# Text queries formed inside the key stage of a two-stream attention block, with the text columns and transposes one group earlier and the key casts given fixed engines

## The chip, the cores and the metric

The kernel runs on one core of one Trainium2 chip. The metric is the device time of one execution in microseconds (us), lower is better. A core has a matrix engine (TensorE, called PE in the profile, with its weight loads listed apart as PEld), VectorE (DVE), ScalarE (ACT), GpSimd (POOL) and SyncE (SP, which here only issues DMA transfers). Each engine runs its own instructions in the order in which the program lists them, and waits on semaphores for the others.

## The reference

Two batches of 256 image tokens and 32 text tokens with D = 1152 features go through one joint attention block. Everything is bfloat16.

```
mod_i = (silu(c) @ wmod_img).reshape(B, 6, 1, D)      # shift, scale, gate used; same for text
hi = layernorm(x_img) * (1 + sci) + shi
ht = layernorm(x_txt) * (1 + sct) + sht
qi, ki, vi = split(hi @ wqkv_img);  qt, kt, vt = split(ht @ wqkv_txt)
q, k, v = concat([text, image], tokens)
p = softmax(q @ k^T * D ** -0.5);   a = p @ v;   at, ai = split(a)
out_i = x_img + gai * (ai @ wo_img)
out_t = x_txt + gat * (at @ wo_txt)
```

## The kernel before

Features are cut into KT = 9 tiles of 128. `hT_i` holds the normed image tokens transposed (features on partitions, 512 tokens), `hT_t` the same for the 64 text tokens. The order on every engine is the order in which the program is written; there is no scheduler. The stages on TensorE follow one another: warm-up, image values together with the image scale columns, image shift columns, image queries, image keys, text queries, text keys, image scores, text scores with the gate rows, text values, transposes of the probabilities, attention times values, then the output products.

Image queries and image keys come out of `qk_img(wq, blk, hooks)`. It walks over seven groups of output tiles: tiles 0 to 2 together, then 3, 4, 5, 6, 7 and 8 alone. A group is 9 matmuls of 128x512 per tile (line 481), each with its own weight load, into one PSUM bank per tile; then the bank is cast to bfloat16 into `qT` or `kT` (line 484). `hooks` maps a tile number to a function that is called ahead of that group, so what the hook issues stands on each engine just before the group's matmuls. In the key stage the hooks are:

- 3, `txt_norm`: the layer norm of the text tokens `x_t` on VectorE and ScalarE, the low part of a shift sum (line 456), and a dummy exponential on ScalarE that has the table loaded early (line 519).
- 6, `row_strips`: three strips of rows on TensorE (text shift `tsh`, text scale `tsc`, and `svr`, the image shift through the value weights), each cast out of PSUM. `svr` goes on through GpSimd to a DRAM scratch and back into `v_t`.
- 7, `all_cols`: six tiny matmuls that turn the strips into columns `ctp`, and four small VectorE instructions that write them to `mod_t` (lines 392 and 394).
- 8, `txt_transposes`: nine matmuls that transpose `x_t` (line 534, tile `tpt`, two PSUM banks), two VectorE products with the scale columns (line 535) and one VectorE addition of the shift columns (line 537), which finishes `hT_t`.

After the last group come the text queries and then the text keys: for each, 81 matmuls of 128x64 with `hT_t` as the moving operand (line 548), in two PSUM banks of 6 and 3 tiles, each cast once. A cast of queries is a ScalarE multiplication by the softmax scale (line 431); other casts go through `evac`, which takes VectorE and ScalarE in turn (lines 156 and 158). By that turn the image key casts of tiles 0, 2, 4 and 7 are on ScalarE and those of 1, 3, 5, 6 and 8 on VectorE, with `tsh` and `svr` on ScalarE and `tsc` on VectorE.

PSUM has one pool `ps_mm` of seven banks handed out in turn, and one bank `ps_sm`. Weights come in tiles of 2592 KB through a pool of five, all issued by SyncE in one fixed order (lines 412 to 422: image keys, text shift, text scale, `x_t`, text queries, text keys, image gate, text values in three parts, image output, text gate, text output in three parts); a load waits until the last reader of the tile whose place it takes is done, and the loads behind it in the queue wait with it.

Of the kernel before, what the change touches and what calls it, by code (L numbers as in the profile page):

```python
# [14 lines left out]
def kernel(  # L15
# [14 lines left out]
    nc = tc.nc  # L30
# [4 lines left out]
    B, NI, D = x_img.shape  # L35
# [19 lines left out]
    act = ctx.enter_context(tc.tile_pool(name="act", bufs=1))  # L55
# [17 lines left out]
    def load_w(src, c0, ksplits=((0, KT),), home=None):  # L73
        t = wpool.tile([P, KT, D], bf, tag="w", name="t") if home is None else act.tile([P, KT, D], bf, tag=home, name="w_home")
        for (k0, k1) in ksplits:
            nc.sync.dma_start(t[:, k0:k1, :], w_view(src)[:, k0:k1, c0:c0 + D])
        return t
# [73 lines left out]

    evac_idx = [0]

    def evac(out_ap, in_ap):
        if evac_idx[0] % 2 == 0:
            nc.vector.tensor_copy(out_ap, in_ap)
        else:
            nc.scalar.copy(out_ap, in_ap)  # L158
        evac_idx[0] += 1
# [191 lines left out]
    def v_rest_out(i0, i1, ps):  # L351
        evac(v_i[:, i0:i1, NM:D], ps[:])
# [14 lines left out]
    def strip_rows(wt, lhs):  # L367
        gps = ps_mm.tile([P, RC + P], f32, tag="mm")
        for kt in range(KT):
            for g in range(NGG):  # L370
                nc.tensor.matmul(gps[32 * g:32 * g + 32, 0:RC], lhsT=lhs[:, kt, :], rhs=wt[:, kt, g * RC:(g + 1) * RC],  # L371
                                 start=(kt == 0), stop=(kt == KT - 1), tile_position=(0, 32 * g))
        for kt in range(KT):
            g = kt % NGG
            nc.tensor.matmul(gps[32 * g:32 * g + 32, RC:RC + P], lhsT=lhs[:, kt, :], rhs=wt[:, kt, NGG * RC:D],
                             start=(kt < NGG), stop=(kt + NGG >= KT), tile_position=(0, 32 * g))
        return gps

    def rows_for_cols(wt, nm, lhs=None):
        gps = strip_rows(wt, sT32 if lhs is None else lhs)  # L380
        g_sb = work.tile([P, RC + P], bf, tag={"shr": "svr", "tsc": "garow2", "tsh": "of"}[nm], bufs=1, name=nm)
        evac(g_sb[:], gps[:])
        return g_sb

    def select_cols(g_sb, cps):
        for c in range(2):
            nc.tensor.matmul(cps[:, c * NGG * B:(c + 1) * NGG * B], lhsT=g_sb[:, c * P:(c + 1) * P],
                             rhs=sel8[:].rearrange("p g b -> p (g b)"), start=True, stop=True)
        nc.tensor.matmul(cps[:, NCOL:NCOL + B], lhsT=g_sb[:, RC:RC + P], rhs=sel2[:], start=True, stop=True)

    def cols_out(dst, cps, add):
        nc.vector.tensor_scalar_add(dst[:, 0:KT - 1, :].rearrange("p (g c) b -> p c g b", c=2),
                                    cps[:, 0:NCOL].rearrange("p (c g b) -> p c g b", c=2, b=B), add)
        nc.vector.tensor_scalar_add(dst[:, KT - 1, :], cps[:, NCOL:NCOL + B], add)
# [17 lines left out]
    w_k_i = load_w(wqkv_img, D, K3)  # L412
    w_sh_t = load_w(wmod_txt, 0)
    w_sc_t = load_w(wmod_txt, D)
    nc.sync.dma_start(x_t[0:P:P // NTT, :], xt_flat[:, :])
    w_q_t = load_w(wqkv_txt, 0)
    w_k_t = load_w(wqkv_txt, D)
# [8 lines left out]
    saccs = [act.tile([P, D], f32, tag=t, name="sacc") for t in ("K", "sacc")]  # L426
    qkTs = [act.tile([P, KT, B, NTOK], bf, tag="Q", name="qT")]

    def qk_evac(out_ap, in_ap, blk):
        if blk == 0:  # L430
            nc.scalar.mul(out_ap, in_ap, SCALE)  # L431
        else:
            evac(out_ap, in_ap)

    sparts = {}

# [21 lines left out]
    def shift_strip():  # L458
        gps = ps_mm.tile([P, RC + P], f32, tag="mm")
        terms = [(n, b) for b in range(B) for n in range(2)]  # L460
        for m, (n, b) in enumerate(terms):
            for g in range(NGG):
                nc.tensor.matmul(gps[32 * g:32 * g + 32, 0:RC], lhsT=ones32[:, b, :], rhs=sparts[n, b][:, g * RC:(g + 1) * RC],
                                 start=(m == 0), stop=(m == len(terms) - 1), tile_position=(0, 32 * g))
        for g, (n, b) in enumerate(terms):
            nc.tensor.matmul(gps[32 * g:32 * g + 32, RC:RC + P], lhsT=ones32[:, b, :], rhs=sparts[n, b][:, NGG * RC:D],
                             start=True, stop=True, tile_position=(0, 32 * g))
        g_sb = work.tile([P, RC + P], bf, tag="svr", bufs=1, name="svr")
        evac(g_sb[:], gps[:])
        return g_sb  # L470

    def qk_img(wq, blk, hooks):

        groups = [(0, 3)] + [(j, j + 1) for j in range(3, KT)]
        for (j0, j1) in groups:
            if j0 in hooks:
                hooks[j0]()
            pss = [ps_mm.tile([P, B * NI], f32, tag="mm", name="qkps") for _ in range(j0, j1)]
            for kt in range(KT):
                for j in range(j0, j1):  # L480
                    nc.tensor.matmul(pss[j - j0][:], lhsT=wq[:, kt, j * P:(j + 1) * P], rhs=hT_i[:, kt, :],  # L481
                                     start=(kt == 0), stop=(kt == KT - 1))
            for j in range(j0, j1):
                qk_evac(qkTs[blk][:, j, :, 0:NI], pss[j - j0][:].rearrange("p (b n) -> p b n", b=B), blk)

    shift_products(0, 0, KT)
    shift_products(1, 0, 2)
# [8 lines left out]
    strips = {}  # L496

    def row_strips():
        strips["tsh"] = rows_for_cols(w_sh_t, "tsh")
        strips["tsc"] = rows_for_cols(w_sc_t, "tsc")  # L500
        svr = strips["svr"] = shift_strip()
        nc.gpsimd.tensor_scalar(svn[:], svr[:, RC:RC + P], -1.0, 0.0, op0=ALU.mult, op1=ALU.add)  # L502
        for b in range(B):
            nc.gpsimd.dma_start(ssc[b, :].rearrange("(q j) -> q j", q=NGG), svr[b:P:32, 0:RC])
        for g in range(2):
            for b in range(B):
                r = 32 * (2 * g + b)
                nc.gpsimd.dma_start(v_t[r:r + NT, :], ssc[b, g * VW:(g + 1) * VW].partition_broadcast(NT))
# [12 lines left out]
    def all_cols():  # L521
        ctp = ps_sm.tile([P, 2, NCOL + B], f32, tag="sm")
        for k, rows in enumerate((strips["tsh"], strips["tsc"])):
            select_cols(rows, ctp[:, k, :])
        for k in range(2):
            cols_out(mod_t[:, k, :, :], ctp[:, k, :], float(k))

    def txt_transposes():
        pick = ident[:].rearrange("p (t r) -> p r t", r=P // NTT)[:, 0, :]
        hv = hT_t[:].rearrange("p k (b t) -> p k b t", b=B)  # L530
        for k0, k1 in ((0, 5), (5, KT)):
            tpt = ps_mm.tile([P, 5, NTT], f32, tag="mm")
            for kt in range(k0, k1):
                nc.tensor.matmul(tpt[:, kt - k0, :], lhsT=x_t[:, kt * P:(kt + 1) * P], rhs=pick, start=True, stop=True)
            nc.vector.tensor_mul(hv[:, k0:k1], tpt[:, 0:k1 - k0, :].rearrange("p k (b t) -> p k b t", b=B),
                                 mod_t[:, 1, k0:k1, :].unsqueeze(3).to_broadcast([P, k1 - k0, B, NT]))
        nc.vector.tensor_add(hv, hv, mod_t[:, 0, :, :].unsqueeze(3).to_broadcast([P, KT, B, NT]))

    qk_img(w_k_i, 1, hooks={3: txt_norm, 6: row_strips, 7: all_cols, 8: txt_transposes})

    FG = 6
    for blk, wq in enumerate([w_q_t, w_k_t]):
        for j0 in range(0, KT, FG):
            jn = min(FG, KT - j0)
            ps = ps_mm.tile([P, FG, NTT], f32, tag="mm")
            for j in range(j0, j0 + jn):
                for kt in range(KT):
                    nc.tensor.matmul(ps[:, j - j0, :], lhsT=wq[:, kt, j * P:(j + 1) * P], rhs=hT_t[:, kt, :],  # L548
                                     start=(kt == 0), stop=(kt == KT - 1))
            qk_evac(qkTs[blk][:, j0:j0 + jn, :, NI:NTOK],  # L550
                    ps[:, 0:jn, :].rearrange("p j (b n) -> p j b n", b=B), blk)


    qpos = [[0, P, 2 * P], [NT, NT + P, 0]]
# [268 lines left out]
    def out_txt_mm():  # L823
        pss = [ps_mm.tile([P, VC], f32, tag="mm", name="ops") for _ in range(2)]
        for h in range(2):
            for dt in range(KT):
                for g in range(NGG):
                    nc.tensor.matmul(pss[h][32 * g:32 * g + 32, :], lhsT=aT[:, dt, NI + h:NI + NTT:2],  # L828
                                     rhs=w_o_t[:, dt, g * VC:(g + 1) * VC], start=(dt == 0), stop=(dt == KT - 1),
                                     tile_position=(0, 32 * g))  # L830
        return pss
# [19 lines left out]
    pss = out_txt_mm()  # L851
# [36 lines left out]
```

## Time and profile before

| what | value |
|---|---|
| time before, median of 3 runs | 117.55 us (117.52 to 117.86) |
| the profiled execution's own time | 117.92 us |
| its span, first to last instruction | 115.9 us |
| PE busy | 109.1 us (94% of the span), 1223 matmuls |
| DVE, ACT, POOL busy | 76.1, 38.6 and 27.6 us |
| mean DMA rate over the span | 353 GB/s, and 400 to 414 in most slices up to 98 us |
| granted TensorE clock | 0.999 |

The profiled execution is one execution, so its span plus 2.0 us around it makes its own 117.92 us, which is 0.37 us above the median of the runs. Times inside the profile are in us from the first instruction. In a chain of waits each row is a start, a length and the engine, tile and line that held the end of the kernel up at that time. "issue" is time in which an engine waited for nothing that the profile shows.

### The profile page before, as it was taken

The numbers are of one execution on the slowest core, as the hardware profiler recorded it, in microseconds if no ns is written. First come the engines' busy times: TensorE is split into PE (matmuls) and PEld (weight loads), VectorE is DVE, ScalarE is ACT, GpSimd is POOL, SyncE is SP. The second block draws the span as 40 slices with busy tenths as digits, with TensorE's granted clock in tenths as the row PEclk, the third lists the DMA queues.
The fourth block names the chain that finished last, engine by engine and source line by source line (L and its number), as shares of the span: only waits on it lengthen the run. The fifth ranks groups of instructions, "written<-read, shape, count | busy, mean of one in ns | idle before, by whom it ended". The sixth has DMA issues, their size and how long they took to land.

```text
span 115.9 us, 2913 instructions
## 1 busy us (share of the span) xinstructions
PE 109.1 (94%) x1223; PEld 64.9 (56%) x1230; DVE 76.1 (66%) x152; ACT 38.6 (33%) x91; POOL 27.6 (24%) x60
## 2 busy tenths in 40 slices
PE   5998999999999999999999999869999999999990
PEld 1354664544944444444448458857688655667660
DVE  1698920452499999999999854026665802998670
ACT  2829660343360620920039421305565700001000
POOL 7000102540130000000000406000460460799200
PEclk9999999999999999999999999999999999999999
DMA  3999999999999999999999999999999999932042
GB/s 87 270 348 371 373 382 402 410 411 413 403 411 413 405 413 405 410 413 411 411 413 414 403 410 408 405 397 408 411 407 404 407 409 400 339 148 102 25 161 68
DMA packets 22775, 40.87 MB, mean 353 GB/s; under 512 B 1311, under 2 KB 6571, under 8 KB 22763
## 3 DMA queue, kind: packets, MB, share of 16 engines
q1 hardware_dynamic: 21680, 39.64, 89.6%
q0 software_dynamic: 608, 0.88, 2.1%
q10 hardware_dynamic: 475, 0.18, 0.6%
q8 instruction: 9, 0.15, 0.5%
q14 instruction: 3, 0.02, 0.0%
HBM read 39.36 MB, written 1.34 MB: 351 GB/s over the span
## 4 chain that ended last, share of the span: by engine, by line
PE 86%; DMA 6%; SPq 2%; issue 2%; DVE 1%
PE qkps L481 30%; PE ps L810 15%; PE va L247 10%; DMA x_i<-in_x_img_dram 6%; PE aps L718 5%; PE ps L548 4%; PE sps L574 4%; PE gps L371 3%; PE ops L828 2%; PE ps L347 2%; SPq L93 2%; PE ps L398 2%; PE ps L649 2%; PE mps L207 1%; PE gps L783 1%
## 5 line engine op out<-in xcount | busy, mean ns | idle before, releaser
L481 PE MATMUL qkps<-hT_i,t 128*128 128x512 bf16 x158 | 35.4, 379 | 0.2
L481 PEld LDWEIGHTS <-t 128*128 128x128 bf16 x162 | 15.6, 98 | 18.4 <-issue 0.2
L443 DVE SCALAR_TENSOR_TENSOR sacc<-w_v_i,mod_img,sacc 128x1152 f32<-128x1152 bf16 x16 | 22.7, 1418 | 0.5
L810 PE MATMUL ps<-t,aT 128*128 128x384 bf16 x99 | 16.4, 326 | 0.0
L810 PEld LDWEIGHTS <-aT 128*128 128x128 bf16 x117 | 11.0, 98 | 6.8 <-issue 0.5
L247 PE MATMUL va<-w_v_i,hT_i 128*128 128x512 bf16 x60 | 14.1, 379 | 0.5 <-DMA w_v_i<-in_wqkv_img_dram 0.3
L816 DVE TENSOR_TENSOR tmp<-ps,gb 128x384 bf16<-128x384 f32 x11 | 6.1, 551 | 6.1 <-PE ps L810 6.1
L247 PEld LDWEIGHTS <-hT_i 128*128 128x128 bf16 x63 | 5.9, 97 | 7.0 <-POOL hT_i L231 0.5
L794 POOL TENSOR_TENSOR w_og<-t,gb 128x384 bf16<-128x384 bf16 x9 | 8.7, 996 | 4.6 <-PE ps L810 4.6
L502 POOL TENSOR_SCALAR svn<-svr 128x128 bf16<-128x128 bf16 x1 | 0.3, 300 | 32.3 <-ACT svr L158 32.3
L165 DVE BATCH_NORM_STATS2 stats<-x_i 128x6 f32<-128x384 bf16 x12 | 5.9, 544 | 2.9 <-DMA x_i<-in_x_img_dram 2.9
L142 PE MATMUL wps<-wz 128*128 128x512 bf16 x16 | 6.5, 562 | 1.2 <-DVE wz L127 1.2
L431 ACT ACTIVATE qT<-qkps 128x512 bf16<-128x512 f32 x9 | 4.9, 596 | 6.4 <-PE qkps L481 6.4
L447 ACT CAST shi<-sacc 128x1152 bf16<-128x1152 f32 x2 | 2.3, 1152 | 13.7 <-DVE sacc L443 13.7
L548 PE MATMUL ps<-hT_t,t 128*128 128x64 bf16 x162 | 5.1, 193 | 1.4 <-issue 1.4
L231 POOL TENSOR_SCALAR hT_i<-hT_i,mod_img 128x256 bf16<-128x256 bf16 x5 | 2.5, 513 | 15.9 <-ACT rstd L172 9.3
L548 PEld LDWEIGHTS <-t 128*128 128x128 bf16 x162 | 4.9, 98 | 1.8 <-issue 1.7
L731 DVE TENSOR_SCALAR aT<-aps,sv 128x288 bf16<-128x288 f32 (+2 forms) x11 | 4.3, 455 | 2.0 <-PE aps L718 2.0
L817 DVE TENSOR_TENSOR o<-tmp,x_i 128x384 bf16<-128x384 bf16 x11 | 4.7, 426 | 0.4
L733 ACT ACTIVATE aT<-aps,sv 128x288 bf16<-128x288 f32 (+2 forms) x11 | 4.0, 468 | 2.2 <-PE aps L718 2.2
L718 PE MATMUL aps<-pT,v_i 128*128 128x288 bf16 (+2 forms) x44 | 4.8, 264 | 0.0
L574 PE MATMUL sps<-kT,qT 128*128 128x288 bf16 x36 | 4.6, 286 | 0.0
(166 smaller groups left out, 146.1 us busy)
## 6 DMA issues: line engine op xcount, KB each, us to landing
t<-in_wmod_txt_dram SPq DMA_DIRECT2D x3, 2592.0 KB, 21.9
t<-in_wqkv_img_dram SPq DMA_DIRECT2D x6, 864.0 KB, 13.1
t<-in_wqkv_txt_dram SPq DMA_DIRECT2D x2, 2592.0 KB, 18.2
t<-in_wmod_img_dram SPq DMA_DIRECT2D x3, 864.0 KB, 11.7
w_home<-in_wmod_img_dram SPq DMA_DIRECT2D x1, 2592.0 KB, 14.4
t<-in_wqkv_txt_dram SPq DMA_DIRECT2D x3, 864.0 KB, 14.0
t<-in_wo_img_dram SPq DMA_DIRECT2D x1, 2592.0 KB, 17.9
t<-in_wo_txt_dram SPq DMA_DIRECT2D x3, 864.0 KB, 15.8
```

Source lines behind the costliest of these rows:

```text
L142: nc.tensor.matmul(ps[:], lhsT=wz[:, 0:P], rhs=wz[:], start=True, stop=True)
L165: nc.vector.bn_stats(stats[0:np_, k, :], x_ap[:, k * CH:(k + 1) * CH])
L247: nc.tensor.matmul(ps[:], lhsT=hT_i[:, kt, i * P:(i + 1) * P], rhs=w_v_i[:, kt, half * VW:(half + 1) * VW], start=(kt == 0), stop=(kt == K ...
L431: nc.scalar.mul(out_ap, in_ap, SCALE)
L443: nc.vector.scalar_tensor_tensor(saccs[b][:], w_v_i[:, kt, :], ap, saccs[b][:], op0=ALU.mult, op1=ALU.add)
L481: nc.tensor.matmul(pss[j - j0][:], lhsT=wq[:, kt, j * P:(j + 1) * P], rhs=hT_i[:, kt, :], start=(kt == 0), stop=(kt == KT - 1))
L548: nc.tensor.matmul(ps[:, j - j0, :], lhsT=wq[:, kt, j * P:(j + 1) * P], rhs=hT_t[:, kt, :], start=(kt == 0), stop=(kt == KT - 1))
L574: nc.tensor.matmul(sps[:], lhsT=qkTs[0][:, ft, b, q0:q0 + P], rhs=qkTs[1][:, ft, b, :], start=(ft == 0), stop=(ft == KT - 1))
L718: nc.tensor.matmul(bank[:, off:off + c1 - c0], lhsT=lhsT, rhs=rhs, start=(first[id(bank)] == n), stop=(final[id(bank)] == n))
L794: nc.gpsimd.tensor_mul(w_og[:, dt, 0:CH], w_o_i[:, dt, NG0:D], gb[:, B - 1, NG0:D])
L810: nc.tensor.matmul(ps[:, 0:cw], lhsT=aT[:, dt, t0:t0 + P], rhs=rhs, start=(dt == DTS[0]), stop=(dt == DTS[-1]))
L816: nc.vector.tensor_mul(tmp[:, 0:cw], ps[:, 0:cw], gb[:, b, cs])
```

## The change

`evac` takes an engine, and the image key casts follow a fixed list: tiles 0, 2, 4, 5, 6 and 7 on ScalarE, tiles 1, 3 and 8 on VectorE. Against the turn before, tiles 5 and 6 move from VectorE to ScalarE; tile 7 stays there. `tsh` and `svr` are named for ScalarE and `tsc` for VectorE, as the turn had them. The transposes of the text move from the hook ahead of tile 8 to the hook ahead of tile 7, right behind the columns. The text queries become a function and move from behind the last image group to the hook ahead of it (tile 8). The text keys stay where they were. No matmul, cast or transfer is added or taken away.

```diff
-    def evac(out_ap, in_ap):
+    def evac(out_ap, in_ap, eng=None):
+        if eng is not None:
+            (nc.vector.tensor_copy if eng == "dve" else nc.scalar.copy)(out_ap, in_ap)
+            return
         if evac_idx[0] % 2 == 0:
...
-    def rows_for_cols(wt, nm, lhs=None):
+    def rows_for_cols(wt, nm, lhs=None, eng=None):
...
-        evac(g_sb[:], gps[:])
+        evac(g_sb[:], gps[:], eng)
...
-    def qk_evac(out_ap, in_ap, blk):
+    K_ENG = ("act", "dve", "act", "dve", "act", "act", "act", "act", "dve")
+
+    def qk_evac(out_ap, in_ap, blk, eng=None):
         if blk == 0:
             nc.scalar.mul(out_ap, in_ap, SCALE)
         else:
-            evac(out_ap, in_ap)
+            evac(out_ap, in_ap, eng)
...
-        evac(g_sb[:], gps[:])                      # svr, in shift_strip
+        evac(g_sb[:], gps[:], "act")
...
-                qk_evac(qkTs[blk][:, j, :, 0:NI], pss[j - j0][:].rearrange("p (b n) -> p b n", b=B), blk)
+                qk_evac(qkTs[blk][:, j, :, 0:NI], pss[j - j0][:].rearrange("p (b n) -> p b n", b=B), blk, K_ENG[j])
...
-        strips["tsh"] = rows_for_cols(w_sh_t, "tsh")
-        strips["tsc"] = rows_for_cols(w_sc_t, "tsc")
+        strips["tsh"] = rows_for_cols(w_sh_t, "tsh", eng="act")
+        strips["tsc"] = rows_for_cols(w_sc_t, "tsc", eng="dve")
...
-    qk_img(w_k_i, 1, hooks={3: txt_norm, 6: row_strips, 7: all_cols, 8: txt_transposes})
-
     FG = 6
-    for blk, wq in enumerate([w_q_t, w_k_t]):
+
+    def qk_txt(wq, blk):
         for j0 in range(0, KT, FG):
...
+    def cols_and_transposes():
+        all_cols()
+        txt_transposes()
+
+    qk_img(w_k_i, 1, hooks={3: txt_norm, 6: row_strips, 7: cols_and_transposes, 8: lambda: qk_txt(w_q_t, 0)})
+    qk_txt(w_k_t, 1)
```

## The prediction

> **What bounds the kernel now.** I read the page first.
>
> ```profile
> PE 109.1 (94%) x1223; PEld 64.9 (56%) x1230; DVE 76.1 (66%) x152; ACT 38.6 (33%) x91; POOL 27.6 (24%) x60
> ...
> q8 instruction: 9, 0.15, 0.5%
> ...
> PE 86%; DMA 6%; SPq 2%; issue 2%; DVE 1%
> ```
>
> TensorE sets the end: 86% of the chain is matmuls in program order. To reorder matmuls gains nothing by itself; only holes in PE's row count. So the next view is the chain around the change.
>
> ```profile
> 66.27 0.02 PE ctp L389
> 66.29 1.97 PE qkps L481 x9
> 68.25 0.27 PE tpt L534 x9
> 68.52 1.94 PE qkps L481 x9
> 70.47 4.55 PE ps L548 x156
> 75.01 1.41 issue
> 76.43 0.35 PE ps L548 x6
> 76.77 1.35 PE sps L574 x11
> ```
>
> From the columns on, PE has no hole except one: 1.41 us, six matmuls before the end of the text keys. A text matmul takes 4.55 / 156 = 0.0292 us, so 162 of them from 70.47 would end at 75.20; the scores start at 76.77. The hole and the refill behind it cost 1.57 us. "issue" says that no semaphore held it: both operands were there. The DMA view of 74.06 to 74.07 shows what was going on:
>
> ```profile
> DMA packets 1, 0.02 MB, mean 1638 GB/s; under 512 B 0, under 2 KB 0, under 8 KB 0
> ## 3 DMA queue, kind: packets, MB, share of 16 engines
> q8 instruction: 1, 0.02, 550.0%
> ```
>
> A 16 KB packet of the instruction queue starts at 74.07 and takes 0.88 us; PE goes on 1.48 us after its end. Narrow windows place the nine packets at 16.17, 30.35, 42.96, 65.25, 74.07, 80.09, 85.97, 91.95 and 104.55. By then PE had run 237, 523, 686, 1082, 1415, 1537, 1873, 2017 and 2238 instructions (matmuls, weight loads and waits): 2001 over eight packets, 250 each, or 256 if missing records are allowed for. So q8 brings PE's program in blocks of about 256. The hole lies ahead of instruction 1466; blocks then begin at 1466 and every 256 before and behind. I tried when a block is asked for. If that is 46 instructions before PE enters the preceding block, seven of the nine packets start 3.43 to 4.04 us later (mean 3.71). With 60 instructions it is 3.55 to 5.21, with 36 it is 2.53 to 3.84, so 46 fits best. The other two fit the same story: the packet behind the hole starts 3.66 us after PE resumed, and the last, after the weight loads had ended, after 0.83.
>
> So the hole is a code block that came late. From request to use it takes 3.65 + 0.88 + 1.48 = 6.0 us under full DMA load, and the block in use before it was nearly all text matmuls: 256 instructions are 128 pairs, 128 x 0.0292 = 3.7 us.
>
> **The change part by part.**
>
> Text queries ahead of the last image group. The same instructions stand before instruction 1466 in another order, so the block still ends six pairs before the end of the text keys. But the 128 pairs in it are now 75 of text keys, 9 of image tile 8 and 44 of text queries. Before, the request came 23 pairs ahead of the block's first, 5 pairs into the text queries: 70.47 + 5 x 0.0292 = 70.62. After, the text queries start at 68.52, where tile 8 started, and the request comes 14 pairs in: 68.93, which is 1.69 us earlier. The block is usable at 76.43 - 1.69 = 74.74. PE arrives at 68.52 + 81 x 0.0292 + 1.95 + 75 x 0.0292 = 75.02, the same time as before, since the work is only permuted. The hole closes with 0.28 us to spare. With the spread of the seven waits (0.22 less to 0.39 more than this packet's 3.65) what is left of it is 0 to 0.11. Gain 1.57, less 0 to 0.11.
>
> [...]
>
> Transposes ahead of tile 7. On PE they only change places with that group. What must hold is that `hT_t` is finished when the text queries start at 68.52, and its cover is now the 1.94 us of tile 7. The VectorE rows:
>
> ```profile
> 66.20 0.69 DVE L156 CAST kT<-qkps 128x512 bf16<-128x512 f32 x1 [0.52 <-PE qkps L481]
> 66.81 0.17 DVE L392 TENSOR_SCALAR mod_txt<-ctp 128x16 f32<-128x16 f32 x1
> ...
> 67.03 0.15 DVE L394 TENSOR_SCALAR mod_txt<-ctp 128x2 f32<-128x2 f32 x1
> 68.44 0.82 DVE L535 TENSOR_TENSOR hT_t<-tpt,mod_txt 128x320 bf16<-128x320 f32 x2 [1.25 <-PE tpt L534]
> 69.30 0.76 DVE L537 TENSOR_TENSOR hT_t<-hT_t,mod_txt 128x576 bf16<-128x576 bf16 x1
> ```
>
> After the change tile 6's cast is off this row. The columns end on PE at 66.29; with 0.05 us to VectorE (as between PE and the cast at 66.20), the four column writes take 66.34 to 66.71, the products 0.82, the addition 0.80 with its gap: 68.33. PE can start at 68.38, with 0.14 to spare. If the seven instructions did not overlap, their rows sum to 2.31 and give 68.65: a wait of 0.13. I take 0.05, range 0 to 0.15. Had tile 6 stayed on VectorE, its 0.69 us would have stood in front and cost about 0.55; the cast list is needed for this step.
>
> Casts on ScalarE. Tile 5 adds 0.57 us ahead of `tsh`: `tsh` ends at 65.3 instead of 64.82, `svr` at 65.7 instead of 65.21, and PE wants `tsh` at 65.78. Covered by 0.4 us; without that cover, one for one. Tile 6 runs at 66.2 to 66.8 on an idle ScalarE. GpSimd's strip transfers behind `svr` start 0.5 us later, and the four loads of `v_t` behind them, which landed at 77.4, land by 78.0 against a reader at 84.72. Banks: each new order of `ps_mm` takes a bank that was cast by 65 or, for the text keys, 67. Nothing.
>
> SyncE. No DMA moves in program order. Text queries end at 70.89 instead of 72.83 and tile 8 at 72.84 instead of 70.47, so at most one weight load behind them waits about 0.8 us longer than its issue at 72.05, into a queue with 22 us of landing time. Nothing.
>
> More weight switching between 64 and 512 columns: the row shows tile 8 to text at the usual pitch. 0 to 0.1, I take 0.05.
>
> What is late next: everything from the scores on moves 1.5 us up, and data may then be missing. The last third of the text values' weights lands at 81.18 (issue 67.69, 13.5 to landing); PE reads it from 84.01, then 82.45. The last third of the text output weights lands at 102.76; read at 105.37, then 103.80. The next code block: asked for when this one arrives, 74.74, plus 6.0 = 80.74, wanted at 83.20 - 1.57 = 81.63. All hold by 0.9 us or more.
>
> The sum: 1.57 - 0.05 - 0.05 - 0.05 (a mean of the rest of the hole) = 1.42 off the profiled execution's 117.92 (span 115.9 and 2.0 around it) = 116.5. That execution is 0.37 above the median of the runs, so the median goes from 117.55 to 116.1.
>
> **The rivals.**
>
> Part of the hole stays: the request runs further ahead than 46 instructions, or the packet waits over 0.3 us longer than in these rows, or text values or output weights now come last. Left standing 0.4 to 0.9: median 116.4 to 117.2. For it: a margin of 0.28 is thin. Chance 0.13.
>
> The hole isn't closed: the packets of 74.07, 80.09, 85.97 and 91.95 are 6.0 us apart, as if the loaded DMA paced them by time. Then the block comes at 76.43 whatever PE does: 117.5. Against it: 65.25 to 74.07 is 8.8, and the packet behind the hole follows PE's restart. [...] Chance 0.09.
>
> Slower, through `hT_t`: PE stops at the first text query until L537 ends. This holds the request back too, so each microsecond of wait costs one. It makes the kernel slower once the chain ends 1.9 us later than 68.38; with 2.5 us the median is 118.2. For it: four more instructions now stand on VectorE between columns and queries, and the cover fell from 0.41 (70.06 to 70.47) to 0.14. Against: VectorE's work in front, the layer norm, tile 3's cast and `tsc`, ends at 65.2, 1.1 us before the columns, and would have to be 3 us late. Chance 0.08, most of it for what I don't see.
>
> **How the numbers follow.** Forecast 0.70, with its own range 115.9 to 116.5. About 0.3%, 0.35 us, is what a measurement of this kernel can tell. The part-closed case is faster by that or more, so faster is 0.70 + 0.13 = 0.83, same 0.09, slower 0.08. The low end 115.8 allows the full 1.57 and 0.2 of the spread of runs; the high end 117.1 takes in nearly all of the part-closed case and leaves out the last two.
>
> **What would show it.** In the changed profile PE has no "issue" row over 0.2 us in the text keys, the text queries start at 68.4 to 68.7 with L537 ended just before, tile 8 runs from about 70.9, and the instruction packet that started at 74.07 starts near 72.4. Scores start at 75.2 to 75.4. A hole of the old size at the same six matmuls would break the reading of the code block; a wait of PE on DVE hT_t L537 would break the cover; waits on weights at L649 or L828 would show that the gain was handed on to the loads.

## The result and the profile after

| | before | after |
|---|---|---|
| median of 6 runs each | 117.81 us (117.52 to 118.22) | 116.40 us (116.22 to 116.69) |
| ratio after / before, 95% interval | | 0.988 (0.9854 to 0.9905) |
| profiled execution, its span | 117.92 us, 115.9 us | 116.51 us, 114.5 us |

The kernel became faster by 1.41 us, as forecast (1.42): 1.2%, where runs of one kernel spread by about 0.3% around their median. The page first: the share of "issue" in the chain that ended last went from 2% to 0%, and VectorE lost two casts to ScalarE.

```profile
span 114.5 us, 2919 instructions
...
PE 108.8 (95%) x1230; PEld 64.7 (56%) x1230; DVE 75.0 (66%) x150; ACT 39.7 (35%) x93; POOL 27.6 (24%) x60
...
PE 87%; DMA 6%; SPq 2%; DVE 1%; issue 0%
```

The chain from the transposes on (start, length, engine, tile and line):

```profile
66.26 0.29 PE tpt L539 x9
66.54 1.96 PE qkps L486 x9
68.50 2.51 PE ps L552 x81
71.01 1.94 PE qkps L486 x9
72.95 2.36 PE ps L552 x81
75.31 4.41 PE sps L585 x36
```

There is no row without a matmul in it. The scores start at 75.31 instead of 76.77, and the gain is all there: 1.46 us. The text keys run their 81 matmuls in 2.36 us without the hole; the text queries take 2.51, 0.15 more, which is a new wait. The DMA view of 72.42 to 72.44 shows the code packet that started at 74.07 before:

```profile
q8 instruction: 1, 0.02, 300.3%
q1 hardware_dynamic: 4, 0.01, 116.2%
```

It starts at 72.43 and ends at 73.39, and the first instruction of its block runs at 74.95.

VectorE's part of the timeline:

```profile
66.30 0.17 DVE L395 TENSOR_SCALAR mod_txt<-ctp 128x16 f32<-128x16 f32 x1 [1.25 <-PE ctp L392]
...
66.72 0.82 DVE L540 TENSOR_TENSOR hT_t<-tpt,mod_txt 128x320 bf16<-128x320 f32 x2
67.58 0.76 DVE L542 TENSOR_TENSOR hT_t<-hT_t,mod_txt 128x576 bf16<-128x576 bf16 x1
```

`hT_t` is finished at 68.34. PE's semaphore instruction for it runs at 68.38 and the first text matmul starts at 68.48, where 68.32 would have been the pitch of tile 7.

### The profile page after: what moved, and what is told of

It is laid out like the page before. It is cut to its first block, busy times and chain, and to the rows that moved or that the text cites. A ratio compares the mean times of both kernels' runs of the same rounds, so it can differ in the third digit from the quotient of the medians.

```text
span 114.5 us, 2919 instructions
## 1 busy us (share of the span) xinstructions
PE 108.8 (95%) x1230; PEld 64.7 (56%) x1230; DVE 75.0 (66%) x150; ACT 39.7 (35%) x93; POOL 27.6 (24%) x60
## 4 chain that ended last, share of the span: by engine, by line
PE 87%; DMA 6%; SPq 2%; DVE 1%; issue 0%
PE qkps L486 31%; PE ps L821 16%; PE va L250 11%; DMA x_i<-in_x_img_dram 6%; PE aps L729 5%; PE ps L552 4%; PE sps L585 4%; PE gps L374 3%; PE ops L839 2%; PE ps L350 2%; PE ps L401 2%; PE ps L660 2%; SPq L93 1%; PE mps L210 1%; PE gps L794 1%; PE tp L193 1%
## 5 line engine op out<-in xcount | busy, mean ns | idle before, releaser
L250 PE MATMUL va<-w_v_i,hT_i 128*128 128x512 bf16 x63 | 14.6, 379 | 0.5 <-DMA w_v_i<-in_wqkv_img_dram 0.5
L142 PE MATMUL wps<-wz 128*128 128x512 bf16 x16 | 5.6, 499 | 1.2 <-DVE wz L127 1.2
L156 DVE CAST kT<-qkps 128x512 bf16<-128x512 f32 x3 | 2.1, 686 | 4.7 <-PE qkps L486 4.7
```

Source lines behind the costliest of these rows:

```text
L142: nc.tensor.matmul(ps[:], lhsT=wz[:, 0:P], rhs=wz[:], start=True, stop=True)
L250: nc.tensor.matmul(ps[:], lhsT=hT_i[:, kt, i * P:(i + 1) * P], rhs=w_v_i[:, kt, half * VW:(half + 1) * VW], start=(kt == 0), stop=(kt == K ...
```

## The experiments

Each time is a median. Each ratio, with its 95% interval, is against the kernel before, run beside it (117.80 to 117.96 us), also where the kernel is a variant of the changed one. A pair is a weight load and its matmul, two PE instructions.

The theory: the hole is a block of PE's program that arrives late, because 256 text instructions (128 pairs of 0.0292 us, 3.7 us) run faster than a block comes (6.0 us from request to use in the kernel before); the change puts nine slow image matmuls (1.94 us) into that block's time. The rivals: something at that place in the program (an operand, a bank, a cast), or code packets paced by time.

**Only the casts.** The hooks of before, with the fixed cast engines:

```diff
-hooks={3: txt_norm, 6: row_strips, 7: cols_and_transposes, 8: lambda: qk_txt(w_q_t, 0)})
+hooks={3: txt_norm, 6: row_strips, 7: all_cols, 8: txt_transposes})
+qk_txt(w_q_t, 0)
 qk_txt(w_k_t, 1)
```

> The order of before with only the fixed cast engines. Theory: nothing, 1.000 of before within 0.3%, with the hole of 1.4 at its place. Rival (the casts free PE or VectorE somewhere on the path): 0.3 us or more faster.

Measured: 117.80, ratio 1.0013 (0.9993 to 1.0033), and a hole of 1.43 us six matmuls before the end of the text keys. The casts alone bring nothing, as expected.

**Casts and transposes, the queries late.**

```diff
-hooks={..., 7: cols_and_transposes, 8: lambda: qk_txt(w_q_t, 0)})
+hooks={..., 7: cols_and_transposes})
+qk_txt(w_q_t, 0)
 qk_txt(w_k_t, 1)
```

> The changed kernel with the text queries put back behind the last image group; the transposes stay ahead of tile 7 and the cast list stays. Theory: the critical block again holds nothing but text matmuls, the hole of 1.4 stays at the same six matmuls and the median is that of before within 0.35 us. Rival (the gain comes from earlier transposes and the cast list): median 116.4 to 116.8 and no hole.

Measured: 117.79, ratio 0.9988 (0.997 to 1.0006). `hT_t` is ready at 68.21 here, 1.9 us before it is used, and the hole stands at the same six matmuls (chain):

```profile
70.30 4.55 PE ps L552 x156
74.85 1.33 issue
76.18 0.35 PE ps L552 x6
```

So the hole isn't `hT_t` either. The gain comes with moving the queries.

**Fewer loads.** The order of before without the last five weight loads:

```diff
-    w_ga_i = load_w(wmod_img, 2 * D, home="V")
-    w_v_t = load_w(wqkv_txt, 2 * D, K3)
-    w_o_i = load_w(wo_img, 0)
-    w_ga_t = load_w(wmod_txt, 2 * D)
-    w_o_t = load_w(wo_txt, 0, K3)
+    w_ga_i, w_v_t, w_o_i, w_ga_t, w_o_t = w_sh_t, w_q_t, w_sc_t, w_k_t, w_q_t
```

> The order of before without the five last weight loads (image gate, text values, image output, text gate, text output); their readers read weights that are there already, so the outputs are not those of the reference. The weight stream then ends at about 68 us, before the critical code block is asked for. Theory (the 6.0 us from request to use are due to the loaded DMA): the packet starts within about 1 us of the request instead of 3.65, the block is usable at about 73 and the hole closes with nothing moved; span 1.4 to 1.8 below before. Rival (the hole is fixed in PE or in the program's place): it stays at six matmuls before the end of the text keys, 1.2 to 1.5 us.

Measured: 116.34, ratio 0.9871 (0.9848 to 0.9893), span 114.5. With nothing moved in PE's order, its DMA is nearly idle from 68 to 76 us, where the DMA of before moved 407 GB/s, and its chain has no hole:

```profile
DMA packets 130, 0.16 MB, mean 21 GB/s; under 512 B 64, under 2 KB 64, under 8 KB 128
```

```profile
68.60 1.94 PE qkps L477 x9
70.54 4.72 PE ps L544 x162
75.27 1.84 PE sps L570 x15
```

The packet starts at 71.72 instead of 74.07, 1.2 us after the point 46 instructions ahead of its preceding block instead of 3.65. So the block is late because of the loaded DMA; how the packet queues inside it isn't shown here.

**Moving the boundary.** Warm-up matmuls are split into smaller ones of the same total width. This adds PE instructions ahead of everything and, if the theory holds, shifts every block boundary by as many, with no other step moved.

```diff
-    warm(11)
+    warm(6)
+    warm_split(5, 4)      # five of 128x512 as 20 of 128x128: 15 pairs more
```

> The order of before, with five of the sixteen 128x512 warm-up matmuls each split into four of 128x128: 15 more matmul and weight-load pairs, 30 more PE instructions, ahead of everything, for the same warm-up columns. Nothing is moved, cast or loaded differently. Theory (the hole is a code block that comes late): every block boundary stands 15 pairs earlier in the program, the request for the critical block now comes while the image group of tile 8 runs at 0.216 us a pair, about 2 us before the old one, and the block is wanted 0.44 us earlier; the hole of 1.41 closes to 0 to 0.3 and the median falls by 1.2 to 1.6, to about 116.3, with the text queries left where they were. Rival (the hole comes from something at that place, or the gain came from moving the queries, the transposes or the casts): the hole stays, six matmuls before the end of the text keys, and the median stays within 0.35 us of before.

Measured: 118.35, ratio 1.0021 (1.0002 to 1.004). Half of it came true and half didn't:

```profile
70.42 4.11 PE ps L556 x141
74.53 1.82 issue
76.36 0.79 PE ps L556 x21
```

The hole moved by exactly 15 pairs, from behind the 156th text matmul to behind the 141st. So the hole goes with the place in PE's program and not with the work done there, as a block boundary would. But the packet started at 74.12, as before, and the hole grew by 0.41, close to the 15 x 0.0292 = 0.44 us by which the block was wanted earlier. So "requested 46 instructions ahead of the preceding block" is not the whole rule. The mended theory is an inference, as no row shows the request itself: PE's sequencer, whose rows in the profile are the instructions that wait for semaphores (PEldq), asks for the block; it runs ahead of the array but stands at an instruction that waits for a semaphore, and in this order it stands ahead of the first text matmul until `hT_t` is done (in the kernel before `hT_t` ends at 70.05, and the sequencer's instruction for it runs at 70.09).

Thirty pairs (ten warm-up matmuls split into four):

> The order of before with ten warm-up matmuls split into four each: 30 pairs, 60 PE instructions more ahead of everything. With 15 pairs the hole moved 15 pairs earlier, as the block boundary did, but its packet started at 74.12 as before and the hole grew by 0.4. Theory, mended: PE's sequencer runs ahead of the array by about 46 instructions and asks for the next block when it enters one, but it does not run past an instruction that waits for a semaphore; the first text matmul waits for hT_t until 70.06, so no request for a block that begins behind it can come before that. With 30 pairs the block begins two pairs ahead of that matmul, inside the image group of tile 8, the request no longer stands behind the wait, and comes 2 us or more earlier: no hole over 0.2 in the text matmuls; 0 to 0.5 may open in attention times values; median 116.3 to 116.9. Rival A (packets are paced by time): packet at 74.1 again, hole grown to about 2.3, median about 118.6. Rival B (the request comes a fixed 46 instructions ahead): would also close it, but is already contradicted by the 15 pairs.

Measured: 118.66, ratio 1.0059 (1.0035 to 1.0083). Missed again: the packet started at 73.81, 0.3 earlier instead of 2.

```profile
70.44 3.67 PE ps L556 x126
74.11 1.97 issue
76.08 1.22 PE ps L556 x36
```

Two pairs ahead of the waiting instruction were not enough; either the request comes some instructions into a block, or packets are paced by time after all. Two more kernels tell these apart. One is the same 30 pairs in the kernel with the early transposes, where the sequencer passes the semaphore sooner:

> The kernel with the transposes ahead of tile 7 and the text queries behind the last image group, plus the 30 pairs in the warm-up. It differs from the 30-pair kernel of before, whose hole was 1.97, only in where the transposes and the two casts stand: PE's semaphore instruction ahead of the first text matmul is passed at about 68.25 instead of 70.07. The block boundary stands at the same 126th text matmul. Theory (the block is asked for when the sequencer gets a few instructions into the preceding block, and the sequencer stands at that semaphore until hT_t is done): the request comes at 68.3 to 68.6, the packet starts at about 72, and the hole shrinks from 1.97 to 0 to 0.5; 0 to 0.4 may open in attention times values. Median 116.3 to 117.0. Rival (the packet comes at about 74 whatever the sequencer does, as in all four kernels whose text matmuls follow tile 8): packet at 73.8, hole about 2, median about 118.6.

Measured: 116.95, ratio 0.9925 (0.9898 to 0.9953). The rows of PE's sequencer at the first text matmul, first for the 30 pairs in the order of before, then with the transposes early:

```profile
L556 PEldq EVENT_SEMAPHORE  x1: 51/51/51, 70.1 to 70.1; - x1
```

```profile
L560 PEldq EVENT_SEMAPHORE  x1: 51/51/51, 68.2 to 68.2; - x1
```

The second sequencer passes the semaphore at 68.17, while its first text matmul runs at 70.06: it works almost 2 us ahead of the array. The first passes it at 70.07, 1.90 us later, and its packet starts 1.90 us later as well, at 73.81 against 71.91. At the same boundary the hole is nearly gone:

```profile
70.22 3.67 PE ps L560 x126
73.90 0.28 issue
74.18 1.22 PE ps L560 x36
```

The other is the order of before with 40 pairs, whose preceding block begins twelve pairs ahead of the waiting instruction (nine warm-up matmuls split into four, one into six, one into nine):

> The order of before with 40 pairs, 80 PE instructions, more in the warm-up. The preceding block now begins 12 pairs ahead of the first text matmul, among the transposes, clearly in front of the semaphore that waits for hT_t. Theory: the request comes at 66 to 68, no hole over 0.3 in the text matmuls; instead 0.4 to 1.0 in attention times values at about 85, where 256 instructions ahead of a boundary that has moved 40 pairs run faster than a block comes; median 116.7 to 117.4. Rival (time-paced packet at about 74): a hole of about 2.3 before the 117th text matmul, median about 119.

Measured: 117.31, ratio 0.995 (0.9921 to 0.9978). The packet starts at 69.64 and 162 text matmuls run in one row:

```profile
68.77 1.94 PE qkps L490 x9
70.71 4.72 PE ps L557 x162
```

So 40 more pairs in the warm-up take the hole of before away without moving a query: 1.97 us at 30 pairs, none at 40. Pacing by time falls. The scores start 1.33 us earlier than before (75.44 instead of 76.77), but 0.38 of that is lost again: a hole of 0.20, expected at 0.4 to 1.0, opens in attention times values, which takes 5.77 us instead of 5.39.

By the mended theory the runs with 30 and 40 pairs in the order of before also place the request. The block begins 4 instructions ahead of the waiting one with 30 pairs, and its packet came behind the wait; with 40 pairs it begins 24 ahead, and the packet came before it. So the request falls between the 4th and the 24th instruction of a block. If it comes when the array is 46 instructions ahead of the block, the sequencer's own lead over the array is about 50 to 70 instructions; that is an estimate from these runs.

The opposite on the changed kernel: 60 pairs more (`warm(2); warm_split(1, 5); warm_split(8, 8)`).

> The changed kernel, with nine of the warm-up matmuls split (one into five, eight into eight) so that 60 more pairs, 120 more PE instructions, stand ahead of everything. Theory: with the boundaries 60 pairs earlier, a block ends in the transposes of the probabilities, behind text scores, gate rows and text values, which run through 256 instructions in about 4.4 us; with 6.0 us from request to use a hole of about 1.6 us (1.2 to 2.0) opens on PE at about 83 to 85, in the transposes, with no transfer or engine to wait for, and the median rises to about 117.9 (117.5 to 118.3). Rival (the order of the text queries itself took the hole away): no hole over 0.3 and a median within 0.35 of the changed kernel's 116.4.

Measured: 118.57, ratio 1.0046 (1.0019 to 1.0073). A hole of 1.31 us, within its range, opens where the boundary was expected to be, between the transposes of the probabilities, in a kernel that has no hole in its text matmuls:

```profile
83.84 0.55 PE pk L678 x8
84.39 1.31 issue
85.71 0.34 PE pk L678 x3
```

The median is above its range of 117.5 to 118.3; the profiled execution took 118.05, and what the rest comes from is not shown.

Counted from the start of the program, 733 weight loads stand ahead of the hole in the kernel before and in every variant with a hole in its text matmuls, with 0, 15 or 30 pairs. In the kernels with 40 and 60 pairs 989 stand ahead of it, though these two holes lie in different stages. The difference is 256 pairs, 512 instructions, two blocks of 256: the holes stand at fixed places in PE's program, whatever runs there. The change is worth its 1.4 us only for the boundaries that this program happens to have.

**The cover of the transposes.** Tiles 5 and 6 back on VectorE:

```diff
-    K_ENG = ("act", "dve", "act", "dve", "act", "act", "act", "act", "dve")
+    K_ENG = ("act", "dve", "act", "dve", "act", "dve", "dve", "act", "dve")
```

> The changed kernel with the image key casts of tiles 5 and 6 back on VectorE, all else as changed. Theory: tile 6's cast of 0.69 us stands on VectorE ahead of the column writes, which begin at about 66.85 instead of 66.30; hT_t is finished 0.5 us later and PE waits for it at the first text query, 0.5 us more than in the changed kernel; the code block's hole stays closed, as the wait holds request and need back alike; median 116.9 (116.7 to 117.1). Rival (the cast list does nothing): within 0.2 of the changed kernel's 116.4.

Measured: 116.99, ratio 0.992 (0.9897 to 0.9944). The cast of tile 6 is on the chain, and PE waits 0.47 us for `hT_t`, as expected:

```profile
66.14 0.69 DVE kT L156
66.84 0.08 DVE mod_txt L395
...
68.03 0.77 DVE hT_t L542
68.80 0.14 issue
68.93 2.52 PE ps L552 x81
```

The transposes back ahead of tile 8, directly before the queries:

```diff
+    def transposes_and_queries():
+        txt_transposes()
+        qk_txt(w_q_t, 0)
-hooks={..., 7: cols_and_transposes, 8: lambda: qk_txt(w_q_t, 0)})
+hooks={..., 7: all_cols, 8: transposes_and_queries})
```

> The changed kernel with the transposes put back ahead of tile 8, so that they stand directly before the text queries with no image group between. Theory: PE has nothing to do from the last transpose at about 68.8 until the three VectorE instructions of hT_t end at about 70.3, a wait of 1.5 to 1.8 on VectorE at the first text query; the code block's hole stays closed, as request and need are held back alike; median 118.0 (117.7 to 118.3), so that the whole gain is handed back. Rival (the wait would have been there anyway inside the code block's time): 116.4 to 117.0.

Measured: 118.30, ratio 1.0048 (1.0029 to 1.0067): 0.5% slower than before. The waits of PE in this stage (engine and tile, for whom, us in total, times, longest):

```profile
PE ps L552 <- DVE hT_t L542: 1.7, 1, 1.7
```

No hole is left in its text keys; the whole gain goes into this wait. The wait holds back request and need alike: the text queries start at 70.13 instead of 68.48, 1.65 us later than in the changed kernel, and the packet at 74.10 instead of 72.43, 1.67 later.

**A version that might beat it.** The text queries behind the second matmul of tile 8's group, beside the changed kernel once more:

```diff
             for kt in range(KT):
+                if kt == 2 and j0 in mids:
+                    mids[j0]()
```

> The changed kernel with the text queries put between the second and third matmul of tile 8's group instead of ahead of it. The first two image matmuls, 0.43 us, stand between the end of hT_t's chain and the first text query. Theory: the 0.15 us that PE waits for hT_t in the changed kernel is covered, and the code block still holds seven image matmuls between text queries and keys; median 0.1 to 0.2 below the changed kernel run beside it. Rival (that 0.15 is the cost of switching between 512 and 64 columns): the same or 0.1 above.

> The changed kernel as it is, to stand beside the others on one chip: 116.4, 0.988 of before.

Measured: 116.94, ratio 0.9905 (0.9879 to 0.9932), and for the changed kernel 116.60, ratio 0.9892 (0.9871 to 0.9913). A gain of 0.1 to 0.2 was expected and didn't come; the intervals overlap, so it isn't shown to be slower either. The profile says why: the wait for `hT_t` is gone, and a hole comes back at the boundary.

```profile
66.85 2.37 PE qkps L488 x11
69.23 2.36 PE ps L554 x81
71.59 0.05 issue
71.64 1.46 PE qkps L488 x6
73.10 2.19 PE ps L554 x75
75.29 0.02 issue
75.31 0.35 PE ps L554 x6
```

The queries take 2.36 instead of 2.51, and the last six text matmuls 0.35 instead of 0.175. From tile 7's start to the scores it is 75.66 - 66.85 = 8.81, against 75.31 - 66.54 = 8.77 in the changed kernel. The two image matmuls that cover the wait are taken from the block's time: the packet starts at 73.09, in the changed kernel beside it at 72.45.

## Why the prediction was right, point by point

- **The hole is a late code block.** Right: it moves pair by pair with the boundary (156, 141, 126 matmuls), it reappears two blocks further on, and it goes when the loads go. The distance of exactly 512 instructions also settles the count of 250 a block in favour of 256. The late block cost 1.57 us of PE in the kernel before under its full weight stream; without that stream no hole was left in the text matmuls.
- **When it is asked for.** The number was right and the rule too simple. The packet was forecast near 72.4 and started at 72.43, 3.57 us after the array came within 46 instructions of the block. One reading was loose: 5 pairs into the text queries of before is 70.42, where the 3.65 is counted from, and not 70.62, as the first text matmul starts at 70.30 and not at the chain's 70.47; the shift of 1.69 came out as 1.64. And by the mended theory the distance of 46 instructions only holds where the sequencer is free. In the kernel of before and in the changed one the block begins 28 and 37 pairs behind the waiting instruction, so that the wait did not bind; with 13 pairs (15 added in the warm-up) it did, and the packet started at 74.12, as before.
- **Gain of 1.57, less 0 to 0.11.** The hole closed entirely, but with less to spare than the 0.28 forecast: the packet ended at 73.39, and with the 1.48 us of before from there to the first instruction the block was usable at 74.87, against 74.95 when PE came to it.
- **Transposes ahead of tile 7, 0.05 taken of 0 to 0.15.** Mis-sized, within its bounds: 0.15. VectorE's end was forecast at 68.33 and came at 68.34. The 0.05 us from VectorE to PE was too short: the semaphore instruction and the start of the matmul took 0.14, from 68.34 to 68.48. With tiles 5 and 6 back on VectorE `hT_t` came 0.45 us later, against 0.55 forecast.
- **Casts on ScalarE, nothing.** Right: `tsh` ended at 65.27 (forecast 65.3), `svr` at 65.65 (65.7), the last load of `v_t` landed at 77.83 (by 78.0).
- **SyncE, nothing.** Right: the next two weight loads went out at 70.19 and 72.37 instead of 69.89 and 72.05, 0.3 us later, and no reader waited.
- **Weight switching, 0.05.** No row of the changed chain shows it: tile 8 takes 1.94 and the text keys 2.36 as before.
- **What is late next, nothing.** Right: from 60 us to the end PE waits for no transfer.
- **The sum.** 116.5 was forecast for the profiled execution and 116.51 measured. That it fits to 0.01 is luck: three terms of 0.05 were taken off, and one of them came to 0.15 and the other two to nothing. The median was forecast 0.3 too low, as it was taken from a median of before of 117.55; over the six runs beside the changed kernel that is 117.81. A sum among the rivals is off as well: `hT_t` 2.5 us late is a wait of 2.36 instead of 0.05, which gives 118.4 and not 118.2.

## What to carry to other kernels

When PE idles with "issue" as the reason, look for an instruction packet that starts shortly before it resumes. In these runs a block took about 6 us from request to use under the full weight stream and was asked for, by the fit, about 300 instructions ahead (the 256 of the block before it and 46 more); where those ran faster, PE stood. A semaphore that PE's sequencer waits for can put the packet off further: by 1.90 us in the two runs with 30 pairs. Put slow matmuls among the fast ones (nine of 0.216 us among those of 0.029 here), or move the boundary, and count what is ahead: an edit that adds PE instructions can open such a hole elsewhere, as 60 pairs in the warm-up did (1.31 us). A step moved up needs its cover counted to the next engine's start, semaphore and first matmul included (0.14 us here from VectorE's end to PE's first matmul).

## What the runs showed of the hardware

- In the two runs with 30 pairs a late semaphore went with a late packet: PE's sequencer passed it 1.9 us ahead of the array with the transposes early (68.17 against 70.06) and at 70.07 in the order of before, with the packet's start as much later (71.91 and 73.81). At the same boundary the hole was 0.28 us with the early semaphore and 1.97 with the late one.
- From the end of a code packet to the first instruction of its block it took 1.3 to 1.5 us where PE was standing (1.28 and 1.33 with 15 and 30 pairs in the warm-up, 1.48 in the kernel before).
- From the request, as the fit places it, to the start of the packet it took 3.4 to 4.0 us for seven of the nine packets of the kernel before, 3.57 us for the changed kernel's packet, both under the full weight stream, and 1.2 us without that stream (fewer loads).
- Small additions far ahead changed the time: in the order of before, 30 pairs in the warm-up made the kernel 0.6% slower, with a hole of 1.97 us in the text matmuls, and 40 pairs 0.5% faster, with none there.
